# An attention and gated-MLP kernel on one core: the written order of all 4,871 recorded units drawn up anew

## The chip, the core and the metric
The kernel runs on one NeuronCore of a Trainium2 chip. Its engines work in parallel, each through its own queue of instructions and in that queue's order: TensorE (PE, and PEld for its weight loads), VectorE (DVE), ScalarE (ACT), GpSimd (POOL) and SyncE (SP), which here issues every DMA. An instruction that waits holds up all that stand behind it on its engine. The metric is the device time of one execution in microseconds (us), the median of three runs.

## The reference, cut to what matters
```
scores  = 0.125 * x @ state.T        # x: 8 batches, 8 heads, 512 x 64; state: 8, 8, 32 x 64
a       = softmax(scores)            # over the 32 states
xread   = a @ state
a2      = softmax(0.125 * state @ x.T)   # over the 512 tokens
sread   = a2 @ x
tokens  = concatenate([xread, sread], per batch)   # 4608 tokens of 512 = 8 heads x 64
out     = ((tokens @ w_a) * (tokens @ w_b)) @ w_out    # 512 -> 1536 (twice) -> 512
```
x, state and the output are float32; the three weights come in as float64 and are turned into float32 on the chip, as part of the kernel.

## The kernel before, in words
Each float32 operand of the large products is split into a rounded high part (names ending in `_h`, a cast on ScalarE) and the rest (`_l`, a subtraction on VectorE), and each product is made of three matmuls of 128x128 by 512 columns (high x high, high x low, low x high). `layer1` (L922) makes two products of the first layer for one of twelve slices of the 1,536 features and one batch of 512 tokens. Each takes one of only two PSUM banks named `ab`: six matmuls (`ab<-at_h,p_h` and the like) fill it. ScalarE copies the first bank out (`a_sb<-ab`), and VectorE multiplies it with the second (`kept_g<-ab,a_sb`). So a bank comes free for the next six matmuls only when that copy or that multiply has read it. `parted` splits the result into `g_h` and `g_l`, and `term` (L1206) or `layer2` (L951) multiplies it with weights of the second layer (`wt`, `wo`) into four PSUM banks `acc`; the sums go to `stg` on VectorE. Finished sums are turned by VectorE (`give`, L841, `turned<-stg`, 128x1024 elements) and stored to `out`. The state tokens go through `States` (L860) at the end (`ab<-xs,sw_st`, then `ms<-wo_st,g_h`).

The first-layer weights are folded with the states once: `project` (L521) makes them (`ms<-wq,sd_h`), and ScalarE's copies `sw` go to DRAM (`scr<-sw`). From there they come back for each batch (`p_raw<-scr`, 512 KB a load) and are split by a ScalarE cast (`p_h<-p_raw`) and a VectorE subtraction (`p_l<-p_raw,p_h`) before `layer1` can use them.

Nothing is issued while this code runs. A `Recorder` (L113) notes each call as a unit with its engine; a few units hold several calls that stay together. There are 2,582 units for TensorE, 1,008 for VectorE, 725 for ScalarE and 556 for SyncE. Then `arranged` (L346) reads the text `ORDER` (L142), a list of all units' numbers in the order in which they are emitted, and L1295 emits them. That line is why every row of the trace carries L1297. Tiles get their buffers in the order in which the list first names them, so the list also decides which of two PSUM banks a product takes. Waits follow from the data and the buffers alone; the list holds no times, yet it was laid out by planned times, so that a unit's place among TensorE's units can be read as the moment at which it was meant to start.

```
        for i in arranged(rec.units):
            for obj, method, args, kw in rec.units[i].calls:
                getattr(obj, method)(*map(real, args), **{k: real(x) for k, x in kw.items()})
```

Units that the prediction names, by their numbers in the list:
- 3000: a matmul `acc<-g_l,wt`; 2994: the VectorE subtraction that makes its `g_l`.
- 2897, 2283, 3538, 2674: each the first matmul of six into an `ab` bank; 2815, 2268, 3519, 2616: the VectorE multiplies (`kept_g<-ab,a_sb`) that free those banks, in that order.
- 4557 and 4565: the first matmuls of two products of the state tokens into `ab`; 4519: a VectorE multiply that frees a bank, 4518: the ScalarE copy that this multiply needs.
- 4816 and 4824: two more such products; 4806: a VectorE addition that frees a bank for one of them, 4767: a turn ahead of it on VectorE.
- 2671: a VectorE subtraction `p_l<-p_raw,p_h`; 2911: `kept_g<-kept_g`, a subtraction.
- 3594: a load `p_raw<-scr`; 3597: the ScalarE cast of what it brings.
- 538, 539 and 553: small VectorE steps of the second softmax (`m<-kept`).

Of the kernel before, what the change touches and what calls it, by code (L numbers as in the profile page):

```python
# [147 lines left out]
138 111 786 221 211 227 217 401 222 218 238 213 139 223 203 208 124 140 1164 196 125 150 200 126 141 156 151-153 142
157-158 154 228 375 389 540 159 239 155 595 162 160 244-245 161 178-179 240 180-182 543 197 163 184-185 183 247 164
246 186 204 190 231 380 187 381 248 386 188 249 189 191 309 1063 205 250-251 268 252 201 165 255 253-254 274 256 192  # L150
257 396 376 209 403 269 258-259 275 271 382 310 377 276 270 265 312 232 72 1052 1072 260-261 277-279 390 233 280 296
281 262 266 283 548 263 302 282 272 25 544 558 391 385 284 311 289 313 387 267 273 285 541 293 392 559 554 314 286-288
1276 290 408 241 1073 315 1053 193 316 320 317 297 411 321 318 322 299 303 1074 323 545 294 234 319 324 264 409 295
412 326 325 1064 1174 395 300 298 330 410 561 327 348 342 235 343 349 397 242 305 578 304 344 785 333 402 1082 579 345
546 350 301 346 336 537 347 351-353 536 334 354 413 562 580 1092 331-332 564 581 583 1075 414 563 1054 339 404 567 355
2527 582 415 337 1065 291 335 338 1058 340 469 366 419 356 472 420 367 292 421 358 470 1077 362 328 422 1083 471 416
565 1084 368 363 417 423 359 586 424 418 341 370 364 369 360 425 361 365 1067 441 568 432 442-443 426 447 405 473 371
435 444 433 372 1055 566 445 398 584 373 448 406 570 449 2530 547 329 1085 450 446 1175 438 357 587 453 571 436 596
572 549 434 451 429 474 597 452 573 1078 430 454 431 475 550 457 588 458 460 1059 461 476 437 477 439 574 1068 440 478
462 479-481 463 1069 598-599 427 1079 482 555 486 306 466 483 502 575 484 1166 551 503 600 1184 464 504 467 2533  # L160
1080-1081 468 2536 589 465 485 822 576 496 505-506 1070 459 821 1104 507 1071 577 487 455 508 556 1105-1106 490 493
590 499 509-510 399 514 591 383 511 30 1107 497 512 1165 513 592 552 214 456 601-602 515 428 491 1102 1167 1108 1087
542 1109 492 498 603 2528 500 585 1103 593 518-519 787 501 229 604 1176 607 663 605 664 666 494 1177 526 608 606 1011
495 609 557 520 5 488 527-528 1024 1094 516 224 665 610 613 611 529 612 522 1093 530 629 667 724 1010 614 630 725 727
631 531 489 620 532 521 1066 728 632 569 635 633-634 621 636-637 617 407 638 1095 622 523 639-640 388 726 641 1185 674
378 618 788 619 533 1179 517 642 615 649 668 650 1089 1086 789 669-670 535 807 1090 671 524 791 1096 675 645 676 672
808 673 677-679 1076 1186 680 525 623 696 646 1118 697 681 698 243 534 805 699 1097 700 702 647 809 624 219 703-704
701 806 705-706 1099 790 1056 1091 1120 648 708 616 626 651 627 1168 707 625 393 2534 1012 729 709 652 1057 730 628
794 657 813 1178 653 658 792 735 11 736 687 810 659 1169 690 737 814 1060 1088 1194 654 682 1266 793 823 655 731 815
738 824 732 1187 691 660 1119 739 797 733-734 825 693 826 643 688 740 694-695 692 827 741 888 656 662 684 1100 798  # L170
1121 685 763 742 686 689 757 721 799 816 661 712 1181 889 683 1018 718 743 1267 890 764-765 719 644 710 758 1110 1171
720 891 715 892 759 722 751 760 713 817 800 1374 766 1098 761 1101 1038 801 716 1111 795 1150 752 1112 767 723 400
1116 717 768 1122 748 714 745 802 1113 1128 744 236 762 1296 803 1189 1117 749 754 818 769 746 1126 755 819 828 804
750 1129 770 1127 753 820 1143 829-830 1114 779 834 771 831-832 1196 835 1268 1013 1115 1130 1170 1123 756 711 833 836
# [14 lines left out]
996 1255 1292 1008 1236 1597 1555 1598-1599 1375 1006 1243 1300 1303 1601 1600 1285 1261 1602-1603 1163 1560 1604 1310  # L189
1355 1260 969 1293 1049 1605 1556 1369 1237 1606 1294 1513 1295 1003 1308 1607 1250 1045 1608 1557 1648 1609-1610 1309  # L190
1843 1558 1009 1611 1566 1612 1512 1613 1561 1290 1314 1614 1514 1685 1262 1620 1050 1621 1738 1256 1386 1257
1622-1624 1563 1356 1304 1625-1626 1802 1627 1302 1628 1156 1315 1311-1312 1629 1632 1562 1263 1324 1651 1305 1251
1564 1526 1630 997 1357 1634 1316 1313 1515 1520 1631 1635 1559 1636-1638 1246 1639 1574 1633 1640 1652 1238 1366 1380
1565 1516 1641 1326 1570 1649 1323 1642 1578 1646 1358 1739 1650 1317 1643 2716 1659 1371 1521 1644 1522 1377 1645
# [1145 lines left out]
```

## Time and profile before
| what | value |
|---|---|
| median of 3 runs (lowest to highest) | 661.97 us (659.99 to 664.33) |
| the profiled execution | 663.3 us, of which the span from the first to the last instruction is 661.5 us |
| granted TensorE clock, mean | 0.996 of full |
| TensorE matmuls busy | 643.4 us, 97% of the span, 3,588 records |
| VectorE busy | 541.2 us, 82%, 1,008 instructions |
| ScalarE busy | 395.5 us, 60%, 742 instructions |
| DMA engines, moved | 170.03 MB, 257 GB/s in the mean |

Busy is the time in which an engine had at least one instruction under way. A matmul's duration is modelled and overlaps the next, so the distance between two starts says what a matmul takes of TensorE. In a timeline row a bracket gives the idle time of the engine just before, and what ended it; "issue" there is a wait for nothing that the profile shows.

### The profile page before, as it was taken

How to read it: one execution, taken by the hardware profiler on the slowest of the kernel's cores; microseconds unless marked ns; L12 is line 12 of the kernel's file. 1: busy time of each engine (PE TensorE's matmuls, PEld its weight loads, DVE VectorE, ACT ScalarE, POOL GpSimd, SP SyncE). 2: the span in 40 equal slices, each digit the busy share in tenths (PEclk: the TensorE clock that was granted, in tenths of full speed). 3: DMA queues.
4: the chain of work that ended last, by engine and by line, in shares of the span. 5: the costliest groups of instructions: out<-in, count | busy, mean ns of one | idle time of the engine just before them, and what ended most of it. 6: DMA issues, size and time to landing. Idle time of an engine off the chain costs nothing.

```text
span 661.5 us, 10316 instructions
## 1 busy us (share of the span) xinstructions
PE 643.4 (97%) x3588; PEld 501.2 (76%) x3588; DVE 541.2 (82%) x1008; ACT 395.5 (60%) x742; POOL 0.7 (0%) x6
## 2 busy tenths in 40 slices
PE   7999999999999999999997999999999999999996
PEld 4676777777878878777876867778787888888785
DVE  5889999976788988899994799989967776676865
ACT  4875965779998866676564454464454364453512
POOL 0000000000000000000000000000000000000000
PEclk9999999999999999999998999999999999999999
DMA  9993577799889999999898869979778446656706
GB/s 327 355 406 120 201 262 249 255 355 311 302 302 320 320 364 317 289 343 268 264 307 270 308 201 305 291 238 282 248 219 255 144 137 177 214 154 209 230 1 159
DMA packets 139763, 170.03 MB, mean 257 GB/s; under 512 B 47808, under 2 KB 97984, under 8 KB 139712
## 3 DMA queue, kind: packets, MB, share of 16 engines
q1 hardware_dynamic: 139712, 169.38, 78.2%
q8 instruction: 28, 0.46, 0.3%
q14 instruction: 23, 0.19, 0.1%
HBM read 114.29 MB, written 55.05 MB: 256 GB/s over the span
## 4 chain that ended last, share of the span: by engine, by line
PE 89%; DVE 5%; DMA 2%; ACT 2%; issue 1%; SPq 0%; POOLq 0%; DVEq 0%; POOL 0%; ACTq 0%
PE ab L1297 42%; PE acc L1297 34%; PE ms L1297 12%; DVE kept_g L1297 1%; DMA wt<-s_dram 1%; DVE turned L1297 1%; DMA raw<-w_out 1%; DMA scr<-sw 1%; DVE m L1297 1%; DVE g_l L1297 0%; DVE s_p L1297 0%; DVE stg L1297 0%; DVE p_l L1297 0%; ACT a_sb L1297 0%; DVE p_raw L1297 0%
## 5 line engine op out<-in xcount | busy, mean ns | idle before, releaser
L1297 PE MATMUL acc<-g_h,wt 128*128 128x512 f32 x504 | 176.0, 393 | 0.2 <-issue 0.2
L1297 ACT COPY a_sb<-ab 128x512 f32<-128x512 f32 (+1 forms) x120 | 68.1, 567 | 148.9 <-PE ab L1297 131.2
L1297 PE MATMUL ab<-at_h,p_h 128*128 128x512 f32 x384 | 148.4, 399 | 5.1 <-DVE kept_g L1297 5.1
L1297 PE MATMUL ab<-at_l,p_h 128*128 128x512 f32 x384 | 147.6, 395 | 0.1
L1297 PE MATMUL ab<-at_h,p_l 128*128 128x512 f32 x384 | 145.9, 392 | 0.1
L1297 PEld LDWEIGHTS acc<-g_h,wt 128*128 128x128 f32 x504 | 94.4, 188 | 20.5 <-ACT g_h L1297 0.6
L1297 PEld LDWEIGHTS ab<-at_h,p_h 128*128 128x128 f32 x384 | 71.9, 188 | 31.3 <-DVE kept_g L1297 8.2
L1297 PE MATMUL acc<-g_l,wt 128*128 128x512 f32 x252 | 94.2, 392 | 0.9 <-DVE g_l L1297 0.9
L1297 PEld LDWEIGHTS ab<-at_l,p_h 128*128 128x128 f32 x384 | 72.4, 188 | 20.5 <-issue 4.8
L1297 DVE TENSOR_TENSOR kept_g<-ab,a_sb 128x512 f32<-128x512 f32 x72 | 49.5, 688 | 43.8 <-PE ab L1297 31.5
L1297 PEld LDWEIGHTS ab<-at_h,p_l 128*128 128x128 f32 x384 | 72.2, 188 | 17.0 <-issue 1.7
L1297 DVE TENSOR_TENSOR g_l<-kept_g,g_h 128x512 fp32r<-128x512 f32 x108 | 72.6, 682 | 4.2 <-ACT g_h L1297 3.3
L1297 ACT CAST g_h<-kept_g 128x512 fp32r<-128x512 f32 x108 | 65.1, 621 | 13.0 <-DVE kept_g L1297 11.9
L1297 PE MATMUL acc<-g_h,wo 128*128 128x512 f32 x192 | 67.4, 392 | 0.0
L1297 DVE TENSOR_TENSOR stg<-acc,stg 128x512 f32<-128x512 f32 x76 | 51.5, 682 | 14.0 <-PE acc L1297 13.2
L1297 DVE TENSOR_TENSOR p_l<-p_raw,p_h 128x512 fp32r<-128x512 f32 x72 | 48.7, 682 | 11.6 <-issue 8.5
L1297 PEld LDWEIGHTS acc<-g_l,wt 128*128 128x128 f32 x252 | 47.3, 188 | 11.3 <-DVE g_l L1297 1.3
L1297 ACT COPY sw<-ms 128x512 f32<-128x512 f32 x72 | 41.5, 589 | 23.5 <-PE ms L1297 14.8
L1297 PE MATMUL ab<-xs,sw_st 128*128 128x512 f32 (+1 forms) x192 | 48.9, 338 | 1.4 <-DVE a_sb L1297 0.7
L1297 ACT CAST p_h<-p_raw 128x512 fp32r<-128x512 f32 x72 | 44.0, 622 | 0.8 <-DMA p_raw<-scr 0.6
L1297 PEld LDWEIGHTS acc<-g_h,wo 128*128 128x128 f32 x192 | 35.9, 188 | 9.3 <-ACT g_h L1297 0.8
L1297 PEld LDWEIGHTS ab<-xs,sw_st 128*128 128x128 f32 x192 | 34.2, 188 | 8.9 <-ACT a_sb L1297 1.5
(130 smaller groups left out, 860.2 us busy)
## 6 DMA issues: line engine op xcount, KB each, us to landing
scr<-sw SPq DMA_DIRECT2D x72, 256.0 KB, 5.0
p_raw<-scr SPq DMA_DIRECT2D x36, 512.0 KB, 5.8
wt<-s_dram SPq DMA_DIRECT2D x36, 512.0 KB, 5.9
wt<-wo_dram SPq DMA_DIRECT2D x54, 256.0 KB, 5.5
raw<-wl SPq DMA_DIRECT2D x24, 512.0 KB, 7.9
x_in<-f_dram SPq DMA_DIRECT2D x36, 256.0 KB, 4.2
out<-turned SPq DMA_DIRECT2D x64, 128.0 KB, 4.3
xn<-xn SPq DMA_DIRECT2D x16, 512.0 KB, 5.1
```

Source lines behind the costliest of these rows:

```text
L1297: getattr(obj, method)(*map(real, args), **{k: real(x) for k, x in kw.items()})
```

## The change
The text `ORDER` is replaced as a whole: the same 4,871 numbers in another order. No unit, operand, size or buffer count is changed, and every engine gets the same instructions. On TensorE half of the units move by at most 5 places and nine tenths by at most 16 (of 2,582), on VectorE by at most 5 and 23 (of 1,008), on ScalarE 3 and 15 (of 725), on SyncE 6 and 24 (of 556). The first 12 units of TensorE and its last 14 keep their places, and so do the last 6 of VectorE, the last 6 of ScalarE and the last 4 of SyncE. The list was laid out again with other assumed durations for VectorE's large turns, for copies with strides and for loads from DRAM; these assumptions stand nowhere in the kernel.

The lines of the list, as it was and as it is, that hold the places spoken of:
```
-6 1 13 7 12 38-39 21 40 26 2 538 41 0 3 127 42 52 9 4 8 10 14 128 66 43-44 53-54 22 45-46 15 47 210 23 16 24 18 55 73
+6 1 7 38 12 39 13 21 40 2 0 26 52 3 41 4 42 8-9 43 10 14 53 44 54 22 45 18 46-47 127 23 15 24 16 55 48 27-28 19 128
...
-2267 2517 2277 2332 2268 2278 2315 2279 2427 1439 2111 2335 1471 2283 2333 2296 2312 2328 2298 2329 2120 2243 2284
+2242-2243 2268 2333 2283 2312 1471 2284 2315 2285 2525 2280-2281 2512 2286 2282 2478 2404 2347 1669 2287 2129 2446
...
-2730 2567 2911 2609 2606-2607 2775 2671 2914 2654 2608 2535 2628 2657 1496 2615 2629 2637-2638 3123 2594 2785 2689
+2637 2731 1486 2797 2911 2702 2662 2656 2630 2614 1496 2638 2567 2639 2671 1487 2775 2657 2692 2673 2529 2663 2658
+2640-2641 2705 2642 2778 2620 2659 2666 2785 2667 2631 2616 2621 2539 2704 2912 2649 2668 2693 2916 2742 2622 2674
...
-2894 2826 2823 2318 2815 2827 2955 2828 2897 2792 2829 2921 2726 2882 2879 2544 2927 2898 2883 2836 2201 2876 2086
+2813 2822 2825 2823 2826 2993 2876 2875 2839 2729 2913 2794 2827 2792 2918 2728 2815 2318 2828-2829 2882 2877 2879
+2951 2919 2878 2722 2897 2840 2836 2929 2917 2830 2795 2831-2832 2796 2898 2896 2302 2833 2975 2930 2834 2977 2921
...
-2936 2980-2981 2961 2737 2982 3250 2962 2986 2983 3219 2846 2984 2987 3184 3273 3089 2994 3000 2988 3141 2991 2860
+2994 3053 2940 2545 2905 2542 2933 2726 2841 2941 2958 2886 2891 3016 2968 2942 2976 2906 2969 1508 2907 2949 2926
...
+3003 3027 3063 3296 2842 2999 3222 2992 2964 3007 2953 2965 3004 3247 3000 3008 2858 3009 2843 3005-3006 3200 3021
+3263 3093 3141 2866 3070 3052 3193 3493 3185-3186 3137 3079-3080 3191 3231 3081-3082 3594 3071 3134 3597 3083 3236
...
-4524 4556 4529-4530 3798 4557 4677 4519 4624 4536 4531 4586 4492 4537 4565 4495 4760 4686 4558 4532 4601 4559 4642
+3797 4537 4493 4584 4519 4530 4565 4495 4566 4603 4567 4601 4568 4550 4531 4557 4617 4558-4559 4618 4560 4751 4605
...
-4819-4821 4773-4774 4806 4668 4731 4824-4825 4740 4807 4826 4822 4808 4739 4669 4827 4598-4599 4823 4775 4771 4828
+4796-4797 4803 4798 4764 4805 4765 4799 4732 4759 4800 4766 4801 4671-4672 4740 4802 4731 4772 4824-4825 4767 4804
+4773 4806 4774 4673 4826 4816-4820 4675 4730 4821-4823 4669 4807 4676 4827 4775 4828-4830 4808 4832 4738 4831 4833
```

## Rows read from the trace of the kernel before

**Rows 1.** The page's busy line: us, share of the span, instructions.
```profile
PE 643.4 (97%) x3588; PEld 501.2 (76%) x3588; DVE 541.2 (82%) x1008; ACT 395.5 (60%) x742; POOL 0.7 (0%) x6
```

**Rows 2.** Timeline of TensorE, 339.4 to 340.6 us: start, us, instruction.
```profile
339.64 0.39 PE L1297 MATMUL ab<-at_h,p_h 128*128 128x512 f32 x1
339.87 0.39 PE L1297 MATMUL acc<-g_h,wt 128*128 128x512 f32 x1
...
340.55 0.39 PE L1297 MATMUL ab<-at_h,p_l 128*128 128x512 f32 x1
```

**Rows 3.** Busy time by stage: length, engines' busy us, clock, DMA share, GB/s.
```profile
0.00:20.00 20.00, 14.99 (x108) 8.71 (x109) 12.29 (x26) 10.72 (x21) 0.70 (x6) 1.00 0.92 325
20.00:340.00 320.00, 318.66 (x1717) 243.98 (x1717) 281.54 (x529) 236.99 (x432) 0.00 (x0) 1.00 0.87 296
340.00:364.00 24.00, 20.61 (x83) 16.05 (x82) 14.14 (x24) 13.36 (x26) 0.00 (x0) 0.93 0.87 271
```

**Rows 4.** Timeline of TensorE: its waits of over 0.4 us after 300 us.
```profile
302.44 0.39 PE L1297 MATMUL ab<-at_h,p_l 128*128 128x512 f32 x1
303.38 0.50 PE L1297 MATMUL ab<-at_h,p_h 128*128 128x512 f32 x1 [0.55 <-DVE kept_g L1297]
...
353.42 0.39 PE L1297 MATMUL acc<-g_h,wt 128*128 128x512 f32 x1
357.19 0.50 PE L1297 MATMUL ab<-at_h,p_h 128*128 128x512 f32 x1 [3.38 <-DVE kept_g L1297]
...
383.12 0.50 PE L1297 MATMUL ab<-at_h,p_h 128*128 128x512 f32 x1 [0.70 <-DVE kept_g L1297]
...
402.94 0.50 PE L1297 MATMUL acc<-g_l,wt 128*128 128x512 f32 x1 [0.89 <-DVE g_l L1297]
...
475.88 0.50 PE L1297 MATMUL ab<-at_h,p_h 128*128 128x512 f32 x1 [0.45 <-DVE kept_g L1297]
...
616.27 0.50 PE L1297 MATMUL ab<-xs,sw_st 128*128 128x512 f32 x1 [0.66 <-ACT a_sb L1297]
...
649.42 0.86 PE L1297 MATMUL ab<-xs,sw_st 128*128 128x512 f32 x3 [0.69 <-DVE a_sb L1297]
```

**Rows 5.** Timeline of TensorE after the longest wait, first and last of eight matmuls.
```profile
358.68 0.60 PE L1297 MATMUL ms<-wq,sd_h 128*128 128x512 f32 x1
...
362.07 0.43 PE L1297 MATMUL ms<-wq,sd_h 128*128 128x512 f32 x1
```

**Rows 6.** Timeline of VectorE around that wait.
```profile
347.51 0.68 DVE L1297 TENSOR_TENSOR kept_g<-kept_g 128x512 f32<-128x512 f32 x1
353.44 0.69 DVE L1297 TENSOR_TENSOR p_l<-p_raw,p_h 128x512 fp32r<-128x512 f32 x1 [5.25 <-issue]
354.05 0.69 DVE L1297 TENSOR_TENSOR kept_g<-kept_g 128x512 f32<-128x512 f32 x1
...
356.45 0.69 DVE L1297 TENSOR_TENSOR kept_g<-ab,a_sb 128x512 f32<-128x512 f32 x1
```

**Rows 7.** Timeline of ScalarE: the cast that VectorE's 353.44 row reads.
```profile
346.92 0.62 ACT L1297 CAST p_h<-p_raw 128x512 fp32r<-128x512 f32 x1
```

**Rows 8.** DMA queues, 348 to 353.4 us: packets, MB, share of 16 engines' time.
```profile
q1 hardware_dynamic: 2048, 1.75, 102.0%
q8 instruction: 1, 0.02, 1.1%
q14 instruction: 3, 0.02, 1.1%
```

**Rows 9.** Timeline of TensorE: the wait at the start.
```profile
16.07 0.64 PE L1297 MATMUL acc<-p_raw,xg 64*32 64x256 f32 x8 [1.50 <-DVE p_raw L1297]
```

**Rows 10.** Timeline of SyncE and of ScalarE: one load `p_raw<-scr` and its cast.
```profile
212.59 0.38 SPq L1297 DMA_DIRECT2D p_raw<-scr  x1
...
219.40 0.62 ACT L1297 CAST p_h<-p_raw 128x512 fp32r<-128x512 f32 x1 [0.56 <-DMA p_raw<-scr]
```

**Rows 11.** The view of the tile `p_raw`: from issue to landing.
```profile
DMA to landing us min/median/max: 3.4/5.7/9.3
```

More of the change, by code (lines that the diff above doesn't have):

```diff
@@ L148 @@
[L148 to L172, printed above, removed]
@@ L190 @@
[L190 to L194, printed above, removed]
@@ new lines @@
+1561 1263 1653-1655 1652 1660 1318 1689 1540 1686 1526 1517 1239 1661 1740 1656 1662 1657 1377 1658 1320 1523 1663
+1665 1325 1687 1319 1571 1579 1264 1671 1664 1672-1673 1568 1674 1666 1675 1572 1324 1562 1541 1574 1332 1580 1321
+1527 1333 1581 1690 1676 1323 1326 1258 1528 1327 1691-1693 1683 1694 1330 1677 1529 1695 1331 1678-1679 1371 1338
+1702 1329 1696 1680-1681 1328 1697 1542 1519 1534 1682 1861 1684 1569 1265 1698 2537 1802 1744 1864 1699 1807 1772
+1718 1339 1573 1530 1334 1700-1701 1745 1376 1704 1370 1705 1763 1719 1336 1525 1761 1703 1706 1337 1381 1543 1575
@@ new lines @@
+1707 1576 1708-1709 1746 1741 1710-1711 1721 1783 1712 1531 1713 1716 1577 1742 1548 1378 1720 1723 1714 1335 1862
+1715 1532 1717 1803 1743 1722 1762 1544 1724 1764 1804 1725 1786 1340 1729 1726 1768 1727 1787 1382 1524 1730 1383
+1350 1874 1808 1765 1728 1809 1341 1784 1731 1735 1769 1732-1733 1747 1770 1360 1734 1805 1736 1342 1533 1766 1748
+1387 1824 1901 1749 1351 1372 1750 1773 1751 1771 1546 1866 1394 1379 1753 1416 1785 1754-1755 1774 1752 1767 1549
+1756 1759 1757-1758 1806 1863 1384 1760 1249 1343 1395 1826 1794 1827 1825 1928 1795 1788 1545 1789 1829 1373 1875
@@ new lines @@
+1796-1797 1550 1790 1428 1389 1798 1791 1865 1920 1830 1779 1535 1799 1792 1867 1668 1780 1793 1344 1879 1781 1800
+1388 1846 1831 1810-1811 1345 1832 1801 1812 1775 1828 1776 1816 1813 1817 1814 1777 1844 1921 1815 1822 1876 1778
+1834 1396 1818-1819 1847 1390 1838 1820 1782 1821 1547 1536 1848 1833 1823 1871 1905 1880 2049 1835 1902 1836 1878
+1392 1868 1353 1849 1869 1839 1837 1850 1906 1851-1852 1393 1877 2057 1922 1872 1840 1853 1909 1859 2008 1854-1855
+1391 1887 2041 1841 1947 1888 1931 1551 1979 1873 1884 1856 1870 1857-1858 1881 1537 1889 1908 2531 1860 1890 1907
@@ new lines @@
+1417 1929 1923 1925 1893-1894 1948 1924 1885 1882 1988 1891 1910 1883 1895 1926 1892 1896-1897 1899 2058 1927 1346
+1912 1911 1898 1991 1969 1886 1408 1932 1913 1419 1949 1916 1933 1952 1930 1539 1934-1935 1900 1398 1917 1980 1950
+1953 1939 1936 1918 1538 1954 1399 1937 1940 1464 1941 1914 1938 1992 2060 1422 1981 1352 1942 1945 1385 1943 2042
+1552 1915 1919 1553 1951 2206 2164 1989 2147 1970 1397 1944 1955 2017 1946 1956-1957 1982 1971 1985 1247 1958-1959
+2148 1990 2007 2050 2009 1960 1400 1983 1975 1993-1994 1986 1967 2016 1995 2165 1987 1996 1976 2059 1961-1962 1997
@@ new lines @@
+1963 2156 2061 2718 1401 1964 1420 1349 1423 1998 1965-1966 1972 2716 1425 1977 1968 1426 1429 1411 1984 2207 1348
+2010 2005 1404 1973 1999-2000 1410 1974 1418 1402 1421 1427 1978 2033 1412 1409 2001 2269 2011 2034 2013 2002 1434
+2003 2035 2004 2077 2036-2037 2018 2076 1403 2006 2012 2167 1431 2014 1347 2015 1465 2027-2029 2078 2112 2030-2031
+2168 2043 2032 2166 2039 2719 2019 2023 2146 1424 2157 2020 2038 2204 2021 2062 2046 2040 2063 1435 2022 2064 2024
+1405 2155 2068 2065 2250 2069 2066 1467 2364 2184-2185 2025 2070 2026 2067 2239 2074 2071 2044 2072-2073 2079 2511
@@ new lines @@
+1444 2179-2180 2327 2125 2220 2090 2118 2107 1443 2182 2208 2221 1413 2293 2222 2091 2126 2092 2223 1445 2127 2214
+1482 2215 2224 2240 1415 1440 2216 1439 2217 1433 2218-2219 2211-2212 2209 1414 2292 2513 2225 2198 2108 2271 1448
+2226 1436 2210 2255 1441 1450 2227 1466 2213 2232 2518 2274 2261 1451 2199 1449 2093 2256 2241 2517 2408 2262 2328
+2094 2190 2294 2235 2522 2263 2313 2335 2236 2346 2311 2237 2257-2258 2233 2272 2131 2273 2427 2297 2259 2295 2314
+2264 1470 2260 2329 2368 2109 2246 2275 2296 2234 2265 2267 2277-2278 2266 2247 2279 2248 2276 2120 2332 1460
@@ new lines @@
+3323-3324 3344 3325 3380 3295 3326 3448 3251 3312 3242 3327 3361 3328 3367 3444 3329 3098 3330 2872 3400 3379 3331
+3456 3418 3396 3332 3104 3415 3401 3364 3116 3333-3334 3252 3335 3397 3117 3336 3420 3368 3550 3449 3345 3313 3346
+3365 3362 3351 3411 3586 3347 3455 3407 3352 3118 3363 3524 3502 3369 3348 3353 3445 3450 3105 3254 3349 3410 3257
+3350 3366 3381 3504 3408 3354 3446 3373 3357 3382 3426 3405 2873 3374 3547 3119 3383-3384 3598 3478 3421 2749 3375
+3385 3355 3406 3447 3386-3387 3575 3413 3120 3440 3398 3370 3458 3427 3402 3356 3394 3371 3464 3595 3409 3376
@@ new lines @@
+3461-3462 3465 3494 3358 3466-3468 3658 3423 3459 3479 3388-3390 3483 3412 3391 3414 3503 3392 3469 3476 3659 3457
+3121 3253 3393 3106 3463 3460 3495 3395 3892 3482 3506 3372 3424 3507 3481 3470 3453 3416 3684 3484 3893 3422 3655
+3471 3810 3752 3508 3576 3498 3419 3509 2624 3425 3472-3473 3122 3258 3428 3474-3475 3499 3510 3505 3656 3477 3429
+3525 4098 3430 3434 3548 3511 3431 3512 3496 3489 3497 3485 3518 3513 3532 3435 3551 3596 3514 3500 2750 3259 3515
+3520 3585 3533-3534 3526 3529 3436 3516 3486 3685 3432 3437 3527 3517 3490 3535 3260 3491 3647 3519 3623 3487
@@ new lines @@
+3626 3612 3633-3634 3642 3651 3814 3753 3635-3637 3572 3638 3686 3629 3645 3643 3687 3627 3661-3662 3711 3644
+3663-3665 3846 3666 3988 3847 3895 3812 3667 3646 3688 3896 3668-3669 3573-3574 3872 3630 2748 3631 3880 3771 3694
+3670-3672 3628 3673 3677 3674 3679 3632 3720-3721 3755 3675 3722 3697 3676 3715 3698 3933 4064 3678 3699 3680 3700
+3723 2635 3701 3716 3681 3703-3705 3791 3690-3691 4010 3706-3707 3815 3702 3849 3712 3708 3682 3729-3730 3709 4006
+3850 3731 3744 3756 3710 3758 3738-3739 3745 3774 3746 3754 3747 3761 2636 3740 3732 3741 4009 3742-3743 3748 3750
@@ new lines @@
+3981 3964 4018 3974 4025 4029 3992 3966 4095 3993 4099 3994 4124 3995 3998-4000 4146 4156 3975 4001 3996 4063 4026
+4184 3997 4125 4147 4358 4002-4003 4030 3971 4166 4091 4004 4032-4033 3982 4034 3972 4035 4005 4038 4047 4092 4036
+3965 4037 4039 4093 4096 4040 4044 4041 4351 4094 4067 4051 4097 4126 4031 4027 4042 4008 4129-4130 3967 4049
+4068-4069 4254 3727 4043 4070 4100 4052 4057 4198 4644 4127 4071 4045 4072 4058 4075 4117 3973 4076 4073 4077-4078
+4074 4079-4080 3976 4083 4168 4081 4233 4082 4109-4111 4084 4271 4167 4128 4059 3968 4086 4028 4103-4104 4370 4105
@@ new lines @@
+4210 4189 4231 4211 3725 4400 4225 4183 4272 4261 4267 4212 4246 4498 4213-4214 4781 4226 4216 4542 4088 4268-4269
+4295 4227 4232 4218 4240 4397 4120 4217 4432 4228 4555 4371 4241-4242 4247 4369 4243 4248 4244 4319 4316 4237 4264
+4245 4249 4238 4252 4359 4250 4265-4266 4320 4251 4431 4275 4538 4276 4360 4423 4234 4291 4253 4296 4219 4089
+4277-4278 4297 4317 4281 4274 4811 4387 4279 4220 4235 4292 4386 4280 4472 4282 4321 4283-4284 3799 4287 4364 4285
+4298-4299 4286 4388 4300-4301 4239 4446 4288 4302-4305 4293 4306 4311 4404 4424 4475 4328 4307-4308 4329 4365 4309
@@ new lines @@
+4318 4556 4330-4331 4294 4332 4401 4310 4405 4312 4333-4335 4361 4236 4670 4473 4580 4355 4491 4366 4402-4403 4336
+4406 4444 4337-4341 4362 4342 4344 4641 4363 4422 4343 4428 4604 4389 4425 4372-4373 4541 4345 4552 4347 4390
+4374-4377 4553 3808 4378-4379 4476 4499 4380-4381 4429 4539 4384 4382-4383 4413 4447 4414 4393 4813 4426 4445 4415
+4385 4540 4394 4407 4398 4391 4430 4433 4408-4409 4642 4410-4411 4416 4520 4412 4448 4392 4427 4419 4503 4395 4417
+4346 4418 4449 4581 4450-4452 4356 4453 4474 4454 4396 4435 4695 4583 4455 4500 4420 4504 4812 4221 4742 4814 4457
@@ L343 @@
+4840 4769 4841 4739 4741 4842 4771 4768 4843-4844 4770 4776 4809 4847 4834 4848 4835 4849 4836 4779 4777 4837-4838
+4845 4854-4856 4850-4851 4780 4852 4778 4861 4866 4862 4857 4863 4859 4867 4860 4858 4868 4864 4869 4865 4870
 """
```

262 lines of the change are left out of this document (113 added, 149 removed), and 27 rows, old and new, of the table ORDER.

## The prediction, made before the changed kernel was run

> **What bounds the kernel now.** I read the page's busy line first, then busy time by stage, then TensorE's timeline wherever it was idle. TensorE has matmuls under way for 97% of the span, VectorE for 82% [rows 1]. Busy overstates a pipelined engine, so the distance between starts is what counts: four 512-column matmuls from 339.64 to 340.55 us stand 0.227 us apart [rows 2], and that is how they stand nearly everywhere. From 20 to 340 us TensorE is busy in 318.66 of 320 us [rows 3]. So it is bound by its own queue, and an order can only give back what TensorE loses in single waits. After the start there are seven of note [rows 4]. Taken as start to start less 0.227 us they are 0.71 us (at 302), 3.54 (353), 0.87 (382), 1.06 (402), 0.61 (475), 0.82 (615) and 0.86 (648); a bracket shows about 0.16 us less, because the last matmul is still draining. They sum to 8.5 us. Five wait for VectorE to free an `ab` bank, one for VectorE's `g_l`, one is put down to ScalarE's copy.
>
> After the longest wait TensorE also runs slowly: eight matmuls from 358.68 to 362.07 us take 3.39 us instead of 8 x 0.227 = 1.82, so 1.57 us is lost [rows 5], in a stage whose granted clock is 0.93 where its neighbour has 1.00 [rows 3]. These are matmuls at the lower of the clock's two levels, 1.2 GHz instead of 2.4.
>
> **What the change moves, part by part.** All engines keep their instructions, so TensorE's own work is unchanged and the terms are waits. I read places in the two lists, counted in TensorE's matmuls between a producer's place and its reader's.
>
> Start: nothing. TensorE's first 12 units are the same, the last of them behind its 1.50 us wait for `p_raw` at 16.07 us [rows 9], and the VectorE steps ahead of that wait keep their sequence. Units 538, 539 and 553 leave VectorE's first 25 us, which could give TensorE a few tenths; I leave that in the range. End: nothing, since TensorE's last 14 units and the other engines' last ones keep their places.
>
> At 402 us, 2994 stood directly ahead of its reader 3000; now 13.5 us of matmuls lie between. All 1.06 us go. At 382, 2815 stood two matmuls ahead of 2897 and now six: 0.9 us more, which covers the 0.87. At 615, multiply 4519 stood behind the matmul 4557 that needs its bank; now 4557 takes another bank, 4519's goes to 4565 behind it, and copy 4518 comes 3.4 us of matmuls ahead of 4557: 0.82 goes. At 648, 4806 stood directly ahead of 4824; now 4816 takes that bank, with 4774, 4673 and 4826 between, two of 512 columns and one of 256, 2 x 0.227 + 0.11: 0.57 of 0.86 goes. At 302, 2268 comes one matmul closer to 2283 (two ahead, now one): 0.23 worse. At 475 three matmuls stay three: nothing. Sum: -1.06 - 0.87 - 0.82 - 0.57 + 0.23 = **-3.1 us**.
>
> That sum looks only where the old list failed; a new list has thin places of its own, and the trace of before cannot show those. I bound them by counting. TensorE steps whose latest VectorE producer stands less than 0.7 us of matmuls ahead number 141 in the old list and 137 in the new; under 1.5 us, 218 and 189 (ScalarE: 135 and 122, 217 and 188). If waits come in proportion to these, a ratio between 0.97 and 0.87, then the six short waits, 4.9 us in all, shrink by 0.15 to 0.65 us only. The ends are -3.1 (no new thin place bites) and -0.15. I take -2, between them, as the four gains are places that I can name.
>
> The wait at 353 us has another cause. VectorE stood idle 5.25 us before 2671 [rows 6], though the cast it reads had started at 346.92 and took 0.62 us [rows 7]; nothing else that the profile shows held it. In that stretch instruction packets (three on q14, one on q8) moved among data that filled the DMA engines to 102% [rows 8]. I read this as VectorE short of instructions behind data. The list has no unit for it. 2671 is VectorE's 566th of 1,008. In the new list the 566th is 2911, and the bank-freeing multiply 2616 is the seventh behind it instead of the fifth: were the shortage to fall on the same number, TensorE would get its bank 2 x 0.6 us later (steps 0.61 apart in rows 6). With other transfers there, it could vanish: 3.54 + 1.57 = 5.1 us less. The term lies between -5.1 and +1.2; I take 0, as the queue is as full and the position as near.
>
> The Trainium skill (Runtime: NRT & Kernel Launch, "Instruction fetch mechanics") says that instructions are prefetched in sequence and that the fetch is hidden by the pace of dispatch. No row here shows such hiding in this stretch, and rows 6 to 8 speak against it. By that rule the 5.25 us would be a wait of the order's own, the new list could well remove it, and the first rival below would be the forecast.
>
> Loads: `p_raw<-scr` takes 3.4 to 9.3 us to land, 5.7 in the median [rows 11]. In the old list one of the 36 has its cast less than 3 us of matmuls behind the issue; in the new list five do (0.5, 1.6, 2.3, 2.3 and 2.6 us). SyncE runs ahead of the list: the load at 212.59 had 2.3 us in the list and 6.81 in the run, the cast having waited 0.56 for it [rows 10], so 4.5 us of head start. With that, a median landing makes only the 0.5 us place (3594, 3597) wait, 0.7 us, and the next ScalarE unit there stands 4.8 us later. So 0, with the slow side below.
>
> Sum: 0 - 2 + 0 + 0 = -2 us. The profiled execution took 663.3 us, 661.5 of span and 1.8 around it, 1.3 above the median of 661.97; the sum makes 661.3 for it and **660.0** for the median. That the three runs lie 4.3 us apart also fits a 5 us stall that some have and some don't.
>
> **Rivals.** (1) A real gain: the shortage of instructions misses the bank's release and no new thin place bites: 661.97 - 5.1 - 3.1 = 653.8. For it: smoother lists (VectorE work above 10 us in each 10 us of TensorE's sums to 14.9 us in the old, 11.3 in the new). Against: DMA stays just as full, and any fetch boundary can be hit.
> (2) Slower, by loads issued too late. Let landings be in the upper half, 7.5 us (between 5.7 and 9.3). The five places then wait 2.5, 1.4, 0.7, 0.7 and 0.4 us, 5.7 in all, on ScalarE, with `a_sb` copies that free TensorE's banks behind them. If TensorE sees all of it and the shortage comes 1.2 us later, that is 661.97 + 6.9 = 668.9; all five at 9.3 would be 14.7 of wait. It decides where a cast waits longer than the distance to the next bank's copy. Against: 4.8 us of room at 3597.
> (3) The redrawing does nothing that counts, and as many new waits open as close: 662.0. For it: 141 thin places against 137.
> A fourth reading gives much more room: the Trainium skill (Perfetto Trace Analysis, "Identifying the Most-Contended Engine") calls matmul busy time a poor measure and takes weight-load busy instead, which is 76% here and would leave 24% of the span, some 160 us by estimate. The matmul starts of rows 2 disagree, and I give it no chance.
>
> **How the numbers follow.** Forecast, -2 us and its ends: 0.54, own range 656 to 665. Rival 1: 0.18. Rival 2: 0.16. Rival 3: 0.12. Within 1%, about what a measurement of this kernel can tell from no change, is 655.4 to 668.6. Rival 1 lies mostly below it (0.15) and the forecast's lower tail adds 0.05: faster 0.20. Rival 2 lies about this edge (0.11), tails add 0.04: slower 0.15. The rest is 0.65. The range goes from half-way into rival 1's tail, 651.5, to rival 2, 669.
>
> **What would show it.** Right: TensorE's starts still 0.227 us apart; no idle before 3000 (`acc<-g_l,wt` near 400 us) and before the first state matmuls near 615; the sum of waits after the start 1 to 3 us less than 8.5. The shortage: VectorE idle for "issue" of several us with its inputs done. Rival 2: ScalarE idle before `p_h<-p_raw`, ended by the DMA, over 2 us. Wrong: a wait of over 1.5 us at a place not named here, or TensorE's starts before 300 us no longer dense.

## The result, and the profile after

The changed kernel took 654.88 us (median of 4 runs, 653.31 to 655.54), the kernel before beside it 662.37: a ratio of 0.9885, 95% interval 0.9848 to 0.9923. Run again later it took 653.79 against 662.04, 0.9881 (0.9856 to 0.9907). So it is faster by a little over 1%. 660.0 was predicted, with a range that holds it; but the likeliest outcome did not come, the first rival's time (653.8) did, and not for that rival's reason. The time lies outside the forecast's own range of 656 to 665, and just past the line of 655.4 that the prediction set for "faster", to which it gave 0.20. The profiled executions, 663.3 and 653.31 us, differ by 10.0, more than the medians, since that of before was a long one and that of after the shortest.

The page's busy line of the changed kernel, against [rows 1]:
```profile
PE 638.9 (98%) x3588; PEld 501.6 (77%) x3588; DVE 541.5 (83%) x1008; ACT 396.1 (61%) x742; POOL 0.7 (0%) x6
```
Busy time by stage of the changed kernel (columns as in [rows 3]: stretch, length, then busy us and number of instructions of TensorE, weight loads, VectorE, ScalarE and GpSimd, granted clock, DMA share, GB/s):
```profile
0.00:20.00 20.00, 15.54 (x110) 9.85 (x111) 11.76 (x24) 10.70 (x21) 0.70 (x6) 0.91 0.83 288
20.00:340.00 320.00, 316.70 (x1711) 242.67 (x1710) 279.48 (x528) 234.75 (x429) 0.00 (x0) 1.00 0.89 299
340.00:364.00 24.00, 24.00 (x107) 19.53 (x108) 19.99 (x35) 16.32 (x31) 0.00 (x0) 1.00 0.89 278
364.00:480.00 116.00, 116.00 (x896) 92.81 (x895) 108.87 (x217) 63.58 (x126) 0.00 (x0) 1.00 0.86 273
...
600.00:651.00 51.00, 46.77 (x222) 38.39 (x220) 38.37 (x67) 15.97 (x33) 0.00 (x0) 0.99 0.47 136
```
Two stretches of the kernel before that [rows 3] doesn't have:
```profile
364.00:480.00 116.00, 113.81 (x879) 89.50 (x878) 106.24 (x213) 58.43 (x117) 0.00 (x0) 1.00 0.85 268
...
600.00:651.00 51.00, 49.65 (x233) 40.45 (x232) 37.64 (x66) 17.10 (x34) 0.00 (x0) 1.00 0.44 136
```
From 340 to 480 us TensorE no longer stands at all (24.00 of 24 and 116.00 of 116; before 20.61 and 113.81), and the clock of 340 to 364 is 1.00 instead of 0.93. From 20 to 340 us TensorE is worse off by 2 us: 316.70 busy instead of 318.66. (From 600 the after row holds less work, because the kernel is nearly done.) All seven waits of [rows 4] are gone. The one long wait that came is in the first half, on TensorE's timeline:
```profile
289.23 0.39 PE L1297 MATMUL ab<-at_l,p_h 128*128 128x512 f32 x1
289.46 0.39 PE L1297 MATMUL ab<-at_h,p_l 128*128 128x512 f32 x1
289.68 0.39 PE L1297 MATMUL ab<-at_h,p_h 128*128 128x512 f32 x1
292.13 0.51 PE L1297 MATMUL ab<-at_h,p_h 128*128 128x512 f32 x1 [2.06 <-DVE kept_g L1297]
```

To sum this up I took, for each of TensorE's 2,582 steps, the distance to the next step's start less the lower quartile for its kind, and call the sum what TensorE loses. The table goes by the place in the list (us of TensorE's work), not by the clock (two expectations below have 14.9, 16.1, 17.3 and 6.2, with quartiles of these two profiles alone):

| | before | after |
|---|---|---|
| first 320 us of work | 14.7 | 15.9 |
| behind it | 17.2 | 6.0 |
| of it: steps that lose over 0.4 us | 6 steps, 7.75 | none |
| of it: steps that lose 0.1 to 0.4 us | 31 steps, 4.9 | 9 steps, 1.2 |
| of it: all others | 4.5 | 4.8 |

So 11.2 us went behind the 320th us and 1.2 came ahead of it, mainly by the new wait at 290: 10 us in all. Of the 11.2, the wait at 353 us and the slow matmuls behind it are 3.54 + 1.57 = 5.1 (the slow matmuls are seven of the 31 steps), the five other waits 4.2, and small waits 4.9 - 1.57 - 1.2 = 2.1. Of these 2.1 some 0.7 still belongs to the six long waits: the first matmul behind such a wait took 0.50 us instead of 0.39 [rows 4], and the next one started 0.11 us later than usual, which makes six more of the 31 steps.

**What VectorE had waited for at 353 us.** In the profile this was "issue". The built program tells more: it lists the semaphores that each instruction waits for.
```
566 L1297 TENSOR_TENSOR p_l_4061<-p_raw_3928,p_h_4046 128x512 [waits DMAHW6_49,DMAHW0_49,Activation_49]
```
That is 2671. Counted through SyncE's DMAs, the first is the load of its `p_raw`, landed at 340.57, and the second is 2194, the last store of a `turned` block: the new `p_l` has the same address as that block and may not be written before the store has read it. SyncE's queue and the landing times of DMAs issued there, in the kernel before:
```profile
347.02 0.43 SPq L1297 DMA_DIRECT2D out<-turned  x1
```
```profile
out<-turned SPq DMA_DIRECT2D x1, 128.0 KB, 6.3
```
347.02 + 6.3 = 353.3 (353.36 by its semaphore in the trace), and 2671 starts at 353.44 [rows 6]. VectorE had turned that block at 295.48; its store stood 50 us behind, and 2.5 us of TensorE's work ahead of 2671. In the new list 2194 is issued at 312.88, and 2671 (the 569th instruction of VectorE, where it was the 566th) takes another buffer and starts without idle time, in a row of two such subtractions:
```profile
352.09 1.28 DVE L1297 TENSOR_TENSOR p_l<-p_raw,p_h 128x512 fp32r<-128x512 f32 x2
```

### The profile page after: what moved, and what is told of

Same layout as the page of the kernel before. It is cut to its first block, busy times and chain, and to the rows that moved or that the text cites. A ratio compares the mean times of both kernels' runs of the same rounds, so it can differ in the third digit from the quotient of the medians.

```text
span 651.4 us, 10339 instructions
## 1 busy us (share of the span) xinstructions
PE 638.9 (98%) x3588; PEld 501.6 (77%) x3588; DVE 541.5 (83%) x1008; ACT 396.1 (61%) x742; POOL 0.7 (0%) x6
## 4 chain that ended last, share of the span: by engine, by line
PE 66%; DMA 2%; DVE 1%; SPq 1%; issue 0%; ACT 0%; DVEq 0%; ACTq 0%
PE ab L1297 33%; PE acc L1297 26%; PE ms L1297 7%; DMA scr<-sw 1%; DMA out<-turned 1%; SPq L1297 1%; DVE kept_g L1297 0%; DVE p_l L1297 0%; DVE g_l L1297 0%; ACT wq L1297 0%; DVE stg L1297 0%; ACT sums L1297 0%; DVE sums L1297 0%; DVE ws L1297 0%; DVE t L1297 0%
## 5 line engine op out<-in xcount | busy, mean ns | idle before, releaser
L1297 PE MATMUL acc<-g_h,wt 128*128 128x512 f32 x504 | 174.2, 392 | 0.1
L1297 PE MATMUL ab<-xs,sw_st 128*128 128x512 f32 (+1 forms) x192 | 50.7, 338 | 0.0
```

## The experiments

First, the wait at 353. SUPPLY is the prediction's reading: VectorE ran short of instructions. BUFFER is the reading found since: 2671 waited for the store that still read the block at its output's address.

**Ten more instructions on VectorE.**
```
         for i in arranged(rec.units):
+            if i == 908:
+                for _ in range(10):
+                    base.vector.tensor_copy(out=ident[:, :1], in_=ident[:, :1])
```


> The kernel before, with ten more VectorE instructions (copies of one column of `ident` onto itself) put ahead of the list's unit 908, where VectorE stands idle 2.39 us at 167 us; everything behind them is ten instructions later in VectorE's stream. SUPPLY (the prediction's reading: VectorE ran short of instructions at its 566th): the idle time of some 5 us near 350 us moves to ten instructions ahead of 2671, or vanishes, and the time is then 657. BUFFER (the rival found since: the program's own waits say that 2671 waits for the store of `turned`, unit 2194, whose buffer its p_l takes; in the profiled execution that store landed at 353.36 and 2671 started at 353.44): the idle time stays ahead of 2671 and ends within 0.1 us of that store's landing, 4 to 6 us of it; the time stays within 1 us of the kernel before.

One run took 662.12 us. Its store, that store's time to landing (a row of the DMA view), VectorE at 2671, now its 576th instruction, and TensorE:
```profile
347.50 0.43 SPq L1300 DMA_DIRECT2D out<-turned  x1
```
```profile
out<-turned SPq DMA_DIRECT2D x1, 128.0 KB, 5.7
```
```profile
353.26 0.69 DVE L1300 TENSOR_TENSOR p_l<-p_raw,p_h 128x512 fp32r<-128x512 f32 x1 [4.47 <-issue]
```
```profile
354.01 0.39 PE L1300 MATMUL acc<-g_h,wt 128*128 128x512 f32 x1
357.01 0.50 PE L1300 MATMUL ab<-at_h,p_h 128*128 128x512 f32 x1 [2.60 <-DVE kept_g L1300]
```
The idle time stayed with the instruction, not with the count: 347.50 + 5.7 = 353.2, and VectorE starts at 353.26. SUPPLY falls.

**The store moved ahead of eight DMAs.**
```
-2193 2532 2576 2599 1461 ... 2797 2578 2565 2573 1486 2579 2194 2697
+2193 2194 2532 2576 2599 1461 ... 2797 2578 2565 2573 1486 2579 2697
```


> The kernel before, with one unit of SyncE's moved: 2194, the last store of a `turned` block, from place 2586 of the list to 2564, directly behind the store 2193; it passes eight other DMAs (7 loads, 1 store). BUFFER: the store is issued at about 343 us instead of 347.0 and lands 3 to 6 us later, at 346 to 349, where VectorE reaches 2671 at 348.2; of the 5.25 us of idle time at most 1 is left, TensorE's 3.54 us wait at 353 and the 1.57 us of slow clock behind it go: 662.2 - 4.5 (4.0 to 5.1) = 657.7. SUPPLY: the idle time stays, 662.

658.78 us against 661.33, 0.9943 (0.9921 to 0.9966). VectorE at 2671, and the stretch on TensorE:
```profile
346.90 0.68 DVE L1297 TENSOR_TENSOR kept_g<-kept_g 128x512 f32<-128x512 f32 x1
347.50 0.69 DVE L1297 TENSOR_TENSOR p_l<-p_raw,p_h 128x512 fp32r<-128x512 f32 x1
```
```profile
340.00:364.00 24.00, 24.00 (x107) 19.09 (x105) 15.51 (x26) 13.87 (x26) 0.00 (x0) 1.00 0.97 294
```
Idle time, wait and slow clock are gone, by one number of 4,871, though DMA is busier than before (0.97). The gain is 2.6 us by the medians, 2.2 to 5.2 by the interval, where 4.5 were expected. In the profiled execution of before the wait cost 5.1 us with the slow matmuls, with ten more instructions 2.8 and no slow clock behind it, so the median may hold less of it than that profile; the runs don't settle this. The edit did more than was meant, however: with the store elsewhere 41 of VectorE's outputs have other addresses, and the stores that 2671's buffer now waits for had landed by 326. So the next one was made.

**The store moved ahead of three loads only.**
```
-2690 2699 2731 2660 2577 2653 2797 2578 2565 2573 1486 2579 2194
+2690 2194 2699 2731 2660 2577 2653 2797 2578 2565 2573 1486 2579
```


> The kernel before, with the store 2194 moved ahead of only three loads of SyncE's (place 2586 to 2575). Every instruction of every engine keeps its buffer, and 2671 still waits for this store; only when it is issued changes, from 347.0 to about 345.3 us. BUFFER: the store lands 1.8 to 2.5 us earlier than 353.36, and VectorE's idle time ahead of 2671 falls from 5.25 us to 2.8 to 3.5, with the end of the idle time still within 0.1 us of the landing; 1.3 to 2.5 us faster than the kernel before, 660.5. RIVAL (the landing is set by what fills the DMA queues, not by the place in SyncE's queue, or VectorE waits for something else): idle time of 4.5 us or more, no change.

659.86 us against 662.81, 0.9958 (0.9932 to 0.9985). Store, landing and 2671:
```profile
343.32 0.42 SPq L1297 DMA_DIRECT2D out<-turned  x1
```
```profile
out<-turned SPq DMA_DIRECT2D x1, 128.0 KB, 5.1
```
```profile
348.64 0.69 DVE L1297 TENSOR_TENSOR p_l<-p_raw,p_h 128x512 fp32r<-128x512 f32 x1 [1.15 <-DMA p_raw<-scr]
```
343.32 + 5.1 = 348.4; 2671 starts 0.2 us behind (0.1 was expected). The bracket names a load, but that load was issued at 344.96 and took 5.7 us, so it landed only after 2671 had started; by the built program's semaphores 2671 waits for its own `p_raw`, landed at 338.93, its cast and this store. The idle time fell further than expected, to 1.15 us, because SyncE was 2 us ahead of the kernel before in this execution, on top of the 1.7 of the place. All engines' buffers are the old ones and only the store's time changed: the landing came 4.9 us earlier and 2671 started 4.8 us earlier. BUFFER is shown.

Second, how much of the gain single places are.

**The four other places repaired.**
```
-2961 2737 2982 3250 ... 3089 2994 3000
+2961 2994 2737 2982 3250 ... 3089 3000
-2926 2894 2826 2823 2318 2815 2827
+2815 2926 2894 2826 2823 2318 2827
-4785 4502 4516 ... 4590 4518 4535
+4502 4516 ... 4590 4518 4785 4535
-4767 4804 4772 ... 4774 4806
+4804 4772 ... 4774 4806 4767
```


> The kernel before, with four units moved by 5 to 13 places, so that the four banks or operands that the prediction names come earlier: 2994 ahead of the turn 2737, 2815 ahead of 2926, the cast 4785 behind the copy 4518, the turn 4767 behind the addition 4806. PLACES (the prediction's sum of terms): TensorE's waits at 402, 382, 615 and 648 us go, 1.06 + 0.87 + 0.82 + 0.86 = 3.6 us: 658.6, with the wait of 3.54 at 353 still there. RIVAL (every moved unit makes another one late): the waits come back at other places, 660.5 to 662.5.

659.70 us against 661.33, 0.9978 (0.9952 to 1.0005): no difference that can be told from none. Busy time of TensorE, TensorE at the old wait and near 407, and VectorE near 407:
```profile
364.00:480.00 116.00, 114.37 (x881) 89.99 (x880) 106.18 (x214) 59.28 (x119) 0.00 (x0) 1.00 0.85 268
...
600.00:651.00 51.00, 51.00 (x243) 42.28 (x242) 38.13 (x67) 17.92 (x36) 0.00 (x0) 1.00 0.44 142
```
```profile
353.85 0.39 PE L1297 MATMUL acc<-g_h,wt 128*128 128x512 f32 x1
358.34 0.50 PE L1297 MATMUL ab<-at_h,p_h 128*128 128x512 f32 x1 [4.10 <-DVE kept_g L1297]
...
406.67 0.39 PE L1297 MATMUL ab<-at_h,p_l 128*128 128x512 f32 x1
407.80 0.50 PE L1297 MATMUL ab<-at_h,p_h 128*128 128x512 f32 x1 [0.73 <-DVE kept_g L1297]
```
```profile
407.06 0.68 DVE L1297 TENSOR_TENSOR kept_g<-ab,a_sb 128x512 f32<-128x512 f32 x1
```
The four waits went: 51.00 of 51 us busy from 600 on, where it was 49.65. But of the 3.6 us taken away behind the wait at 353 only some 2 stayed away: 0.90 came back five us behind the place at 402, 0.34 at 441, 0.39 at 653. Near 407 VectorE has no idle time in either profile. The multiply that frees the next bank starts at 407.06, half a us later than in the kernel before, and TensorE, no longer held at 402, is there 0.7 us earlier. The time lies between the two readings, and so does the account. The wait at 353 is still the store's: it landed at 354.51, and 2671 started at 354.59.

**All five moves.** The diffs of the store among eight DMAs and of the four together.

> Both edits together, five units of 4,871 moved. If the change's gain (654.9 against 662.4, 7.5 us) is these five waits, the two add up: 662.2 - 4.5 - 3.6 = 654.1, as fast as the changed kernel. If the gain comes from the list as a whole (all waits everywhere shorter), the five moves give clearly less, 657 or more.

656.45 us against 661.33, 0.9911 (0.9879 to 0.9943): between the two readings, a gain of 4.9 us of the 7 to 8. TensorE's busy time:
```profile
340.00:364.00 24.00, 24.00 (x108) 19.37 (x107) 15.67 (x26) 14.80 (x28) 0.00 (x0) 1.00 0.91 281
364.00:480.00 116.00, 114.82 (x884) 90.41 (x883) 110.41 (x221) 60.34 (x120) 0.00 (x0) 1.00 0.89 282
```
From 364 to 480 us 1.2 us are still idle, none in the changed kernel. Behind the 320th us it loses 9.1 us against 6.0, in 22 steps of 0.1 to 0.4 us against 9, and in two larger ones (1.5). That remainder belongs to the list as a whole; what in the list makes it, no run here shows.

Third, the halves of the list.

> The changed kernel as it is, beside the kernel before on the same chip as the three below: 654 to 656, a ratio of 0.989 as at first; the profile again shows 2 to 2.5 us of wait near 290 us and no wait over 1 us behind it.

653.79 us, 0.2 below the range expected. Its profile has 1.72 us of lost time at 290 (expected 2 to 2.5) and none over 0.6 behind it.

**Old up to 320 us of TensorE's work, then new; and the reverse.** Nothing but `ORDER` differs: the first list's units up to that place, then the other list without these.

> A list of two halves: all that the old list puts ahead of its 320th us of TensorE's work, in the old order, then the rest in the new order. By the two profiles TensorE loses 14.9 us to all kinds of waiting ahead of that point in the old list and 16.1 in the new, and 17.3 against 6.2 behind it. HALVES ADD UP (the gain lies in the second half, and none of it needs the first): 14.9 + 6.2 = 21.1 us lost against 22.3, 1 us faster than the changed kernel, 653.5. THE LIST IS ONE (a second half is right only behind its own first half, since buffers and loads reach across): 656 or more.

652.94 us against 662.04, 0.9866 (0.9841 to 0.9892), as the sum of halves said.

> The halves the other way round: the new list up to the 320th us of TensorE's work, then the rest in the old order. The store 2194 falls into the new part, so it is early here. HALVES ADD UP: 16.1 us lost in the first half, 17.3 - 5.1 in the second, 28.3 in all against 32.3 of the kernel before: 658, with the short waits of the old list at 382, 402, 475, 615 and 648 back and no idle time of several us of VectorE near 350. SUPPLY (a shortage at VectorE's 566th instruction, whatever the order around it): the 5 us stand there, 662 or more.

662.91 us, 1.0019 (0.9998 to 1.0040): 5 us above the sum of halves, the time that SUPPLY gave, but without its idle time: VectorE has none of over 2.2 us between 295 and 400. What it lost lies elsewhere, on TensorE:
```profile
291.90 0.39 PE L1297 MATMUL ab<-at_h,p_h 128*128 128x512 f32 x1
294.90 0.73 PE L1297 MATMUL ab<-at_h,p_h 128*128 128x512 f32 x1 [2.61 <-DVE kept_g L1297]
295.43 1.05 PE L1297 MATMUL ab<-at_l,p_h 128*128 128x512 f32 x2
...
339.28 0.40 PE L1297 MATMUL acc<-g_h,wt 128*128 128x512 f32 x1
341.23 0.73 PE L1297 MATMUL acc<-g_l,wt 128*128 128x512 f32 x2 [1.55 <-DVE g_l L1297]
```
The wait at 290 is there, longer and with slow matmuls behind it, and at the seam TensorE waits for a `g_l` for which VectorE is late. (This profile is of the longest of the twelve executions, 666.2 us.) Taken as times, the two halves do add up: 652.94 - 662.04 = -9.1 and +0.9 make -8.2, and the whole change made -8.25. The whole gain comes without the new first half.

**The seam at 280 instead of 320.**

> Old order up to the 280th us of TensorE's work, the new one behind it. The stretch from 280 to 320 cost TensorE 1.9 us of waits in the old list and 0.8 in the new one. HALVES ADD UP: 652.9 - 1.0 = 651.9. THE LIST IS ONE: the seam costs as much as it saves, 652.5 to 654.

662.76 us against 662.97, 0.9997 (0.9973 to 1.0021); both readings missed by 9 us. TensorE's busy time around the seam, TensorE, and ScalarE:
```profile
280.00:340.00 60.00, 52.05 (x228) 38.95 (x227) 50.13 (x92) 35.23 (x66) 0.00 (x0) 1.00 0.86 270
```
```profile
304.53 0.39 PE L1297 MATMUL ab<-at_l,p_h 128*128 128x512 f32 x1
307.06 0.50 PE L1297 MATMUL ab<-at_h,p_h 128*128 128x512 f32 x1 [2.14 <-ACT a_sb L1297]
```
```profile
304.50 0.62 ACT L1297 CAST g_h<-kept_g 128x512 fp32r<-128x512 f32 x1 [4.27 <-PE acc L1297]
```
ScalarE stood 4.27 us before a cast whose buffer a matmul still read, and the copies that free banks stood behind the cast. A seam is not free: here two lists that are each dense lose 8 us in 60. So the adding up at 320 is a result for that place only.

Fourth, the waits that the new list still has, and a faster one.

**Two stores earlier in the new list.** Unit 1413 ahead of 2205, unit 1031 directly behind 1030.

> The changed kernel with two stores moved up in its list: 1413 (`scr0_1<-sw`) from place 2151 to 2071, ahead of four loads and a group of three, and 1031 (`s_dram1<-ws_l`) from place 1095 to 1058. BUFFER: the longest waits that the new list still has are of the same kind as the old one's, a buffer that a store still reads: the multiply 2182 at 291.39 us started 0.12 us after the landing of 1413 at 291.27, the subtraction 871 at 157.31 started 0.10 us after that of 1031 at 157.21. With the stores early, TensorE's waits of 2.23 us (at 290) and 0.64 us (at 159) go: 2 to 2.8 us faster than the changed kernel, 652.5, the fastest so far. RIVAL (SyncE's order is zero-sum: the loads that stand behind the moved stores are now late): waits of the same size on `a`, `wt` or `p_raw` come near 290 us, no gain.

652.98 us, 0.9865 (0.9839 to 0.9891) against before; 0.8 below the changed kernel in the same runs (653.79), less than the two intervals can tell apart. TensorE at a new wait, and where the old one was, near 290:
```profile
195.55 0.39 PE L1297 MATMUL ab<-at_h,p_h 128*128 128x512 f32 x1
196.78 0.50 PE L1297 MATMUL ms<-wq,sd_h 128*128 128x512 f32 x1 [0.85 <-ACT sw L1297]
...
290.31 0.39 PE L1297 MATMUL acc<-g_l,wt 128*128 128x512 f32 x1
290.54 0.39 PE L1297 MATMUL ab<-at_h,p_h 128*128 128x512 f32 x1
```
The waits at 290 and 159 are gone (BUFFER), and 1.0 us at 195, 0.8 at 169 and 1.1 at 298 came. The rival's sum was right (no gain that can be told from none), though not by the loads that it named.

**A store made late.** In the list of two halves:
```
-2194 ... 2193 ... 1461
+... 2193 ... 2194 1461
```


> The list of two halves (old to 320 us, then new; 652.9 when it ran), with one unit moved: the store 2194 from place 2500 to 2539, behind the stores and loads that SyncE has there. In this list the bank-freeing multiply 2505 (place 2543) takes the buffer that 2194 reads; in its profile 2194 was issued at 333.94 and landed at 337.62, and 2505 started at 340.09. BUFFER: issued about 7 us later and landing 4 to 6 us after that, at 345 to 347, the store makes 2505 wait 5 to 7 us instead of 1.5, and TensorE with it, as the bank is its next: 4 to 6 us slower than without the move, 657 to 659, more where the clock falls behind the wait. RIVAL (such a wait is absorbed, other work is there for TensorE): within 1 us of 652.9.

652.69 us, 0.9866 (0.9832 to 0.9900): no cost. The premise failed, not the mechanism: once the store was moved, the allocation gave 2505 another buffer, whose DMAs had landed by 323.4, and 2505 waited for its copy alone:
```profile
339.44 0.69 DVE L1297 TENSOR_TENSOR kept_g<-ab,a_sb 128x512 f32<-128x512 f32 x1 [0.77 <-ACT a_sb L1297]
```
This says nothing on what a late store costs; it says that the place of a store decides who gets its buffer, so that the order in which tiles are first named, as told ahead of the prediction, is not all that decides.

**The list of two halves with three units moved.**
```
-2192 ... 2194 ... 2193
+2192 2193 2194 ...
-2297 ... 2268
+... 2268 2297
```


> The list of two halves with three units moved in its old part: the stores 2193 and 2194 directly behind 2192 (place 2404), about 25 us earlier, and the turn 2297 (0.70 us) from ahead of the bank-freeing multiply 2268 to behind it. BUFFER and PLACES: the 0.7 us that 2505 waited for the store 2193 and the 0.62 us wait of TensorE at 303 go: 652.9 - 1.1 = 651.8. RIVAL: the 0.5 us by which SyncE's loads come later, or the turn, costs as much elsewhere: 652.5 to 653.5.

651.14 us against 662.97, 0.9847 (0.9815 to 0.9879), the lowest median here, 11.8 us less than the kernel before (8 to 12 by the interval). Its six runs lie at 650.85 to 653.42, those of the changed kernel at 652.74 to 655.46. The bank's multiply at the seam and TensorE near 302:
```profile
337.76 0.69 DVE L1297 TENSOR_TENSOR kept_g<-ab,a_sb 128x512 f32<-128x512 f32 x1 [0.71 <-ACT a_sb L1297]
```
```profile
302.02 0.39 PE L1297 MATMUL ab<-at_h,p_l 128*128 128x512 f32 x1
302.50 0.50 PE L1297 MATMUL ab<-at_h,p_h 128*128 128x512 f32 x1
```
The multiply, which has another buffer here too, no longer waits for a store, and of the 0.62 us at 302 0.25 is left.

## Why the prediction was right or wrong

**What bounds it: right.** TensorE's starts still stand 0.23 us apart (289.23, 289.46, 289.68), and all that moved was single waits. The start gave nothing, as said, though not by standing still: the wait for `p_raw` fell from 1.5 to 0.6 us, that for `xg` rose from 1.7 to 2.3, and the clock of the first 20 us was 0.91; the first 40 us of work lose some 5 us in both profiles. The rule of the Trainium skill that left room for some 160 us by estimate (Perfetto Trace Analysis, "Identifying the Most-Contended Engine") fits no run here: the fastest list still loses 19 us by the account above, and by that account an order can give back no more.

**The wait at 353: wrong, and the largest single term.** "I read this as VectorE short of instructions behind data" was taken from two things that stood side by side, an idle engine whose inputs were done, and instruction packets between data. The inputs were checked, the output's buffer was not. Ten inserted instructions left the wait where it was, and the store moved ahead of three loads cut it from 5.25 to 1.15 us. With that reading the term could only be a matter of luck (0, between -5.1 and +1.2); with the right one it could have been read from the two lists: 2194 stood 30 places ahead of 2671 in the old and 310 in the new, so a wait for this store had to go. With the other terms as they were that makes 661.97 - 5.1 - 2 = 654.9. That this meets the time is partly luck: its 5.1 is that of one execution in which the clock fell, and its 2 was too small. In the two experiments that moved this store alone the wait was worth 2.6 and 2.9 us by the medians (2.2 to 5.2 and 1.0 to 4.5 by the intervals), so about half of the 5.1 between the forecast and the result; the rest of the miss is the term for the other places. The sentence of the Trainium skill (Runtime: NRT & Kernel Launch, "Instruction fetch mechanics") that was set against the trace, that the pace of dispatch hides the fetch, is no longer contradicted by any row here: the idle time that spoke against it was a wait for a store.

**The named places: right in sign, too small.** The four named waits went, as said; of the two that were to stay or grow (0.23 worse at 302, nothing at 475) both went as well. Six waits, 4.9 us, against -3.1, of which the prediction counted 2. Distances between two places in a list were taken for times. At 475 the distance stayed three matmuls and 0.61 us of wait went, which points to how late VectorE runs against the list; the distance doesn't show that, and no run here singles it out. One place was misread: at 615 matmul 4557 took the bank that copy 4518 reads, as its bracket says (`a_sb` of ScalarE, [rows 4]), not that of multiply 4519. In the new list 4557 takes 4519's bank, and 4565, now ahead of it, that of 4518. The wait went all the same.

**New thin places: right in kind, wrong in the bound.** A new wait of 2.2 us came, at a place not named, which the prediction had set down as a sign that it is wrong; it too is a buffer that a store still reads. VectorE's multiply 2182 started 0.12 us behind the landing of 1413, in the changed kernel:
```profile
291.39 0.69 DVE L1297 TENSOR_TENSOR kept_g<-ab,a_sb 128x512 f32<-128x512 f32 x1 [2.71 <-DMA scr<-sw]
```
On the other side the small waits behind 320 us fell. Without the seven slow matmuls and the six steps right behind the long waits they were 18 steps and are 9, and lose some 1.5 us less, where the counts of thin places (141 to 137) allowed 0.15 to 0.65 in all. The count has VectorE's distances to TensorE. It has neither the waits of VectorE for DMA, such as that of 2182, nor its backlog; which of them made the small waits fewer, no run here shows.

**Loads: right for TensorE.** The casts at the five close places found their loads landed. ScalarE's casts `p_h<-p_raw` wait 3.1 us in all for loads, where it was 0.6, most of it at a place that the prediction didn't count:
```profile
275.44 0.62 ACT L1297 CAST p_h<-p_raw 128x512 fp32r<-128x512 f32 x1 [2.23 <-DMA p_raw<-scr]
```
That is over the 2 us that the prediction set as a sign of rival 2, but no wait of TensorE is ended by such a load, and its matmuls near 275 us start without idle time between them.

**The rivals.** The first had the time (653.8) and the condition "the shortage misses the bank's release", which wasn't the cause; its other half, "no new thin place bites", was not met either, and places and small waits that it left out made up for it, so that its time came is luck. The third (nothing) and the second (slower) did not come. The range, 651.5 to 669, holds a gain of 10 us and no change alike; that it held the time says little of the mechanism.

## What to carry to other kernels

When an engine stands idle with its inputs done and the profile names nobody, look at the buffer that it is about to write: list the semaphores of that instruction and the last reader of that address, stores to DRAM above all. In an order written out by hand a store's place decides when a buffer comes free and who gets it; try it first right behind the work that fills the block, and look at the addresses again after each move. Part of what is taken from single waits can come back at the next late step of the engine that frees the buffers (3.6 us taken, some 2 kept): five moves gave 4.9 us here, the whole new list 7.5 to 8.25.

## What the runs showed of the hardware that was not expected

The same wait costs more in some executions than in others. Behind 3.38 and 4.10 us of idle time at 353, and behind 2.61 at 294 in the list new-then-old, TensorE's next matmuls stood some 0.43 us apart instead of 0.227, at the lower of its two levels, 1.2 GHz (granted clock 0.93 in 340 to 364 us of the first two, 0.81 in 291 to 300 of the third); behind 2.60 us at 354 with the ten extra instructions, and 2.06 at 290 in the changed kernel, they did not. It fits the spread of the kernel before (657.2 to 666.9 us over all its runs, 650.85 to 653.42 in the fastest list), but no run was made to show that it is the cause.

The store 2194 of 128 KB, issued at 341 to 348 us in six profiles, took 3.4, 3.8, 5.1, 5.7, 6.3 and 7.2 us to land (five moves, among eight DMAs, among three loads, ten more, before, four moved): at the slow end longer than a load of 512 KB (`p_raw<-scr`, 5.7 in the median). All stores `out<-turned` of the kernel before took 2.0 to 6.9 us, 4.3 in the median.
